# Attention scores of tiles 2 to 4 as three fp32r products

## The chip, the core and the metric

The kernel runs on one core of a Trainium2 chip. A core has five engines with a queue each: TensorE (PE, matmuls; its weight loads are shown apart as PEld), VectorE (DVE), ScalarE (ACT), GpSimd (POOL) and SyncE (SP, which issues DMAs). They share the on-chip memory SBUF; TensorE writes into PSUM, from which VectorE and ScalarE read. The metric is the device time of one launch in microseconds, the median of several runs. A run takes a little longer than its span, which is the time from the first to the last instruction in the trace.

## The reference, cut to what matters

Block-causal attention for 8 batches of 8 heads with 576 positions of 64 numbers, then a mixture of 8 experts of which each position takes one.

```python
scores = scale * np.matmul(q, k.transpose(0, 1, 3, 2))      # scale = 1/8
mask = block_i >= block_j                                   # blocks of 64 positions
scores = np.where(mask, scores, -1000000000.0)
attn = np.exp(scores - np.max(scores, axis=-1, keepdims=True))
attn = attn / (np.sum(attn, axis=-1, keepdims=True) + 1e-09)
x = np.matmul(attn, v)                                      # heads side by side: 4608 rows of 512
...
h = np.maximum(xe @ w1[e], 0.0)                             # the rows of one expert
out[mask] = gate_w[mask, None] * (h @ w2[e])
```

All inputs and the output are float32.

## The kernel before, in words

The kernel has two parts. The first, up to some 360 us, does the attention and the routing (class Attention, class Router); the second does the experts (class Experts) and isn't touched, except that one job which prepares its weights runs in the first part.

**Pairs and tiles.** The attention works on 32 pairs of heads, four to a batch. A pair's two heads lie in the two halves of the 128 partitions, so that a matmul of one head uses 64 rows; they are called a and b. The 576 rows of scores of a head are cut into tile 0 (64 rows, both heads in one matmul, line 160) and tiles 1 to 4 (128 rows each). Tile i needs the keys up to its end: 192, 320, 448 and 576 columns. Tile 4 is written in two matmuls of 288 columns. `op_S` (line 155) issues them, head a and head b by turns, each with the scaled queries `q` as the weights and the raw keys `kd` as the moving operand, in f32. Scores of tiles 1 to 3 go to the PSUM tiles ya and yb, those of tile 4 to xa and xb.

**Steps.** Each step of a pair has a short name: ld (loads qd, kd and v), pQ (scales q by 1/8 on GpSimd, line 114), S (scores), K (mask, VectorE memset), M (maximum, VectorE, line 187), E (exp with sum, ScalarE, line 202), R1 and R2 (sum plus epsilon, line 208, and reciprocal, line 211, on VectorE), Z (scales tile 0 on GpSimd, line 215), T (transposes on TensorE, line 241), H (their copies out of PSUM, on ScalarE, one on VectorE), V (product with v), O (copy of that), F, X and Y (the product with a folded matrix, and the scaling of its rows).

**Order.** The string ORDER (line 416) is the order in which one turn of the loop issues steps; `S4:2` means tile 4 of the pair that is two turns old. So one turn works on five pairs at once, and the 32 pairs take 36 turns. Within an engine the instructions run in that order; across engines semaphores hold them apart. An entry z issues a step of the router, an entry y (`other`, line 1546) takes one job from a list: a scatter of token numbers (line 697, on GpSimd), a gather, or a half of a weight split. There are 8 such splits, of 512 columns each: `first` (line 1510) writes the high part of a piece of w1 in fp32r, `second` (line 1516) the low part, both on GpSimd. The type fp32r is a float32 that is rounded so that one product of TensorE takes it; the experts' matmuls are already done as three products of high and low parts.

## Time and profile before

| | |
|---|---|
| median of 3 runs | 811.13 us (810.02 to 811.5) |
| the profiled execution: time, span | 810.1 us, 808.4 us |
| TensorE busy | 781.2 us, 97% of the span |
| weight loads busy | 592.4 us |
| VectorE, ScalarE, GpSimd busy | 471.8, 400.0, 389.7 us |
| mean granted clock of TensorE | 0.996 of 2.4 GHz |

A row of a timeline names an engine, the line of the kernel, the instruction, what it writes and reads (buffer numbers left out), and the shape. A f32 matmul of TensorE stands as two records. In brackets stands how long the engine had been idle, and what ended that. The ends of matmuls are modelled; the distance from start to start tells what one costs.

### The profile page before, as it was taken

What the parts mean: (1) busy time and instruction counts of PE and PEld (TensorE: products, weight loads), DVE (VectorE), ACT (ScalarE), POOL (GpSimd) and SP (SyncE); (2) the same over time, 40 slices, a digit from 0 to 9 for tenths busy, and PEclk for the clock granted to TensorE, in tenths of its full rate; (3) what the DMA queues carried; (4) which work ended last, traced back from release to release, by engine and by line L of the source; (5) the groups of instructions that cost most, each with busy time, mean ns of one, the idle gap of its engine ahead of it and who ended that gap; (6) DMA issues with size and microseconds to landing.
All of it is one profiled execution on the core that took longest, in us unless ns stands there. A gap on an engine that the chain in (4) does not pass through costs nothing.

```text
span 808.4 us, 17546 instructions
## 1 busy us (share of the span) xinstructions
PE 781.2 (97%) x4524; PEld 592.4 (73%) x4524; DVE 471.8 (58%) x1316; ACT 400.0 (49%) x1016; POOL 389.7 (48%) x397
## 2 busy tenths in 40 slices
PE   4999999999999999998999999999999999999995
PEld 2677666667776666766878888888888888888874
DVE  3566666776776777665855764412144713656963
ACT  3677777777777787772432323322332222323221
POOL 4122243344443362425456776555555555575663
PEclk9999999999999999999999999999999999999998
DMA  5234454646362626442337676744456564677762
GB/s 164 98 101 155 131 149 140 158 135 154 121 167 95 147 86 160 159 107 49 139 110 222 192 237 171 234 134 118 121 150 192 171 185 122 194 223 223 223 207 74
DMA packets 71120, 123.65 MB, mean 153 GB/s; under 512 B 16449, under 2 KB 37697, under 8 KB 70978
## 3 DMA queue, kind: packets, MB, share of 16 engines
q1 hardware_dynamic: 49858, 87.84, 37.4%
q0 software_dynamic: 7680, 20.50, 8.0%
q10 hardware_dynamic: 13440, 13.78, 6.3%
q8 instruction: 45, 0.74, 0.4%
q14 instruction: 97, 0.79, 0.4%
HBM read 73.09 MB, written 21.98 MB: 118 GB/s over the span
## 4 chain that ended last, share of the span: by engine, by line
PE 93%; POOL 2%; ACT 1%; issue 1%; DMA 1%; ACTq 1%; DVE 1%; DVEq 0%; POOLq 0%
PE py L1172 25%; PE o L272 12%; PE pt L1011 11%; PE ya L171 7%; PE o L1011 7%; PE ph L1011 7%; PE xa L171 5%; PE o L307 4%; PE o L301 1%; ACT pb L202 1%; PE o L160 1%; ACTq L1122 1%; DMA xg<-xd,idx 0%; POOL low L1145 0%; POOL tab L697 0%
## 5 line engine op out<-in xcount | busy, mean ns | idle before, releaser
L1172 PE MATMUL py<-w,low 128*128 (+1 forms) x912 | 217.3, 394 | 3.3 <-POOL low L1145 2.0
L1172 PEld LDWEIGHTS py<-w,low 128*128 128x128 f32 x912 | 172.0, 189 | 41.6 <-POOL low L1145 2.5
L114 POOL TENSOR_SCALAR q<-qd 128x640 f32<-128x640 f32 x32 | 58.0, 1811 | 186.7 <-PE o L160 133.4
L1190 ACT ACTIVATE y<-py,gates 128x512 f32<-128x512 f32 x35 | 24.1, 689 | 184.6 <-issue 129.5
L1145 POOL TENSOR_TENSOR low<-high,low 128x512 fp32r<-128x512 f32 x69 | 97.3, 1433 | 12.1 <-ACT low L1137 11.5
L980 POOL TENSOR_TENSOR xl<-high,xh 128x512 fp32r<-128x512 f32 x33 | 45.7, 1385 | 109.8 <-ACT xh L970 109.8
L1089 DVE STREAM_TRANSPOSE hblk<-xg 128x512 f32<-128x512 f32 x35 | 24.8, 709 | 87.9 <-DMA xg<-xd,idx 84.6
L202 ACT ACTIVATE pb<-ya,neg 128x320 f32<-128x320 f32 (+2 forms) x96 | 50.1, 525 | 48.1 <-DVE neg L187 48.1
L1011 PE MATMUL pt<-w,xh 128*128 x272 | 70.8, 392 | 0.0
L1333 DVE TENSOR_TENSOR w<-raw,w 128x1024 f32 x48 | 68.0, 1456 | 0.0
L1330 DVE CAST w<-raw 128x1024 f32 x48 | 56.8, 1222 | 16.0 <-issue 12.6
L171 PE MATMUL ya<-kd,q 64*128 64x192 f32 (+2 forms) x192 | 61.8, 456 | 2.7 <-ACT pb L202 2.7
L171 PE MATMUL yb<-kd,q 64*128 64x192 f32 (+2 forms) x192 | 61.8, 456 | 0.0
L1011 PEld LDWEIGHTS pt<-w,xh 128*128 128x128 f32 x272 | 51.0, 188 | 11.1
L697 POOL DMA_INDIRECT tab<-toks,posi x40 | 41.5, 1037 | 28.8 <-DVE run L664 14.8
L918 POOL DMA_INDIRECT xg<-xd,idx x39 | 44.0, 1128 | 19.3 <-POOL idx L910 17.2
L202 ACT ACTIVATE pb<-yb,neg 128x192 f32<-128x192 f32 (+2 forms) x96 | 49.8, 526 | 0.2 <-DVE neg L187 0.2
L1137 ACT CAST low<-high 128x1024 fp32r<-128x1024 f32 x35 | 36.6, 1045 | 26.5 <-DMA high<-hblk 26.5
L1101 DVE STREAM_TRANSPOSE hblk<-pt 128x512 f32<-128x512 f32 x34 | 23.4, 705 | 43.4 <-ACT pt L1048 43.4
L171 PE MATMUL xa<-kd,q 64*128 64x288 f32 x128 | 41.6, 447 | 6.6 <-POOL q L114 6.6
L307 PE MATMUL o<-fold,oT 128*128 128x144 f32 x256 | 43.9, 294 | 1.1 <-ACT oT L279 0.6
L187 DVE TENSOR_REDUCE neg<-yb 128x1 f32<-128x192 f32 (+2 forms) x96 | 42.8, 474 | 3.3
(1013 smaller groups left out, 1775.1 us busy)
## 6 DMA issues: line engine op xcount, KB each, us to landing
raw<-w SPq DMA_DIRECT2D x52, 512.0 KB, 4.9
high<-hblk SPq DMA_DIRECT2D x280, 48.0 KB
high<-hblk ACTq DMA_DIRECT2D x280, 48.0 KB
qd<-qT SPq DMA_DIRECT2D x32, 352.0 KB, 3.1
v<-vt SPq DMA_DIRECT2D x32, 352.0 KB, 4.8
kd<-kT SPq DMA_DIRECT2D x32, 288.0 KB, 3.8
xd<-xt SPq DMA_DIRECT2D x7, 1026.0 KB, 8.9
xd<-xg SPq DMA_DIRECT2D x9, 256.5 KB, 7.0
```

The lines of the kernel that those rows point to most:

```text
L114: self.nc.gpsimd.tensor_scalar(q, self.raws[m][0][:, 0 : 512 + P], 0.125, None, ALU.mult)
L171: ins = mm(out, q[r, 128 * (i - 1) : 128 * i], k[r, o : o + n], start=True, stop=True, skip_group_check=True)
L202: ins = self.nc.scalar.activation(dst, src, AF.Exp, bias=self.neg[m][:, c : c + 1], scale=1.0, accum_out=self.sums[m][:, c : c + 1])
L272: self.nc.tensor.matmul(out[r], self.raws[m][2][:, slot], self.ph[m, bank][:, c0:c1], start=t in (0, 5), stop=t in (4, 5), skip_group_chec ...
L307: mm(t[:, i], self.oT[m, 0][:, o : o + P], w, start=True, stop=True)
L918: pool.indirect_dma_start(out=self.xg[i], out_offset=None, in_=self.xd[:, :], in_offset=bass.IndirectOffsetOnAxis(ap=self.idx[:, t : t + 1 ...
L980: pool.tensor_sub(xl, r, xh).then_inc(sem["xp"], 1)
L1011: m = pe.matmul(ph[f], x[:, P * k : P * k + P], weights(k, f, part), start=start and k == 0, stop=stop and k == 3,)
L1145: engine.tensor_sub(hl[:, c], h[:, c], hh[:, c]).then_inc(sem["ln" if engine is pool else "le"], 1)
L1172: m = pe.matmul(self.py[t % 2], h[:, c // 4, P * (c % 4) : P * (c % 4) + P], wf[:, bass.ds(off + (base + 512 * c), 512)], start=n == 0, st ...
L1330: dve.tensor_copy(part(c, 0), raw[c % 4]).then_inc(sem["wh"], 1)
L1333: dve.tensor_sub(part(c, 1), raw[c % 4], part(c, 0)).then_inc(sem["wd"], 1)
```

## The change

- Pairs 2 to 31 get the scores of tiles 2, 3 and 4 in fp32r. Their queries and keys are split into a high part (rounded to fp32r) and a low part (the rest, in fp32r), and each f32 matmul becomes three: high by high, high by low, low by high, summed in PSUM. Tile 1, tile 0 and the first two pairs stay f32.
- `gQ` (GpSimd) scales the 384 columns of q for tiles 2 to 4 into the high part; `lQ` (GpSimd) subtracts it from q in three pieces of 128 columns. `gK` (ScalarE) copies the 576 columns of the keys into their high part; `lK` (GpSimd) subtracts it in four pieces of 144.
- In ORDER, pQ moves from behind S0 to behind Z and a new entry y2, with gQ and lQ behind it. gK and lK stand behind the last copy of the transposes (Hx3@A).
- A third entry y takes one more job from the list per turn, until the list is empty.
- The two halves of a weight split are each two instructions of 256 columns instead of one of 512.
- Three tile pools are added, two with two buffers each, and one of 64 bytes that nothing uses.

```diff
--- before.py
+++ after.py
@@ -57,6 +57,9 @@
         self.raw = ctx.enter_context(tc.tile_pool(name="araw", bufs=3))
         self.rawv = ctx.enter_context(tc.tile_pool(name="arawv", bufs=5))
         self.spl = ctx.enter_context(tc.tile_pool(name="aspl", bufs=2))
+        self.hk = ctx.enter_context(tc.tile_pool(name="ahk", bufs=2))
+        ctx.enter_context(tc.tile_pool(name="apart", bufs=1)).tile([P, 16], F32, tag="apart", name="apart")
+        self.hq = ctx.enter_context(tc.tile_pool(name="ahq", bufs=2))
         self.pt = ctx.enter_context(tc.tile_pool(name="apt", bufs=9))
         self.sm = ctx.enter_context(tc.tile_pool(name="asm", bufs=3))
         self.ot = ctx.enter_context(tc.tile_pool(name="aot", bufs=2))
@@ -65,7 +68,7 @@
         self.ps_t = ctx.enter_context(tc.tile_pool(name="pst", bufs=2, space=PSUM))
 
         self.cp, self.ident = cp, ident
-        self.raws, self.qs = {}, {}
+        self.raws, self.qs, self.hilo = {}, {}, {}
         self.pb, self.sums, self.neg, self.rs = {}, {}, {}, {}
         self.bank, self.ptile, self.ph, self.oT, self.xs = {}, {}, {}, {}, {}
         self.small_bank, self.at = (None, None), {}
@@ -113,6 +116,33 @@
         q = self.qs[m] = self.spl.tile([P, 512 + P], F32, tag="q", name=f"q{m}")
         self.nc.gpsimd.tensor_scalar(q, self.raws[m][0][:, 0 : 512 + P], 0.125, None, ALU.mult)
 
+    def high_low(self, m, k, n):
+
+        pool = self.hk if k == "k" else self.hq
+        self.hilo[m, k] = [pool.tile([P, n], F32R, tag=k + x, name=f"{k}{x}{m}") for x in "hl"]
+        return self.hilo[m, k][0]
+
+    def op_gQ(self, m):
+
+        if m > 1:
+            self.nc.gpsimd.tensor_scalar(self.high_low(m, "q", 384), self.raws[m][0][:, P:512], 0.125, None, ALU.mult)
+
+    def op_lQ(self, m):
+        if m > 1:
+            hi, lo = self.hilo[m, "q"]
+            for c in range(0, 384, P):
+                self.nc.gpsimd.tensor_sub(lo[:, c : c + P], self.qs[m][:, P + c : 2 * P + c], hi[:, c : c + P])
+
+    def op_gK(self, m):
+        if m > 1:
+            self.nc.scalar.copy(self.high_low(m, "k", S), self.raws[m][1])
+
+    def op_lK(self, m):
+        if m > 1:
+            hi, lo = self.hilo[m, "k"]
+            for c in range(0, S, 144):
+                self.nc.gpsimd.tensor_sub(lo[:, c : c + 144], self.raws[m][1][:, c : c + 144], hi[:, c : c + 144])
+
     def banks(self, m, x):
 
         if (m, x) not in self.bank:
@@ -160,18 +190,25 @@
             mm(self.part(1, m, "S0", 432, 496), q[:, 512:], self.raws[m][0][:, 512 + P :], start=True, stop=True)
             return
         e = 64 + 128 * i
+        at = P * (i - 1)
+        terms = ((q, k),)
+        if m > 1 and i > 1:
+            (qh, ql), (kh, kl) = self.hilo[m, "q"], self.hilo[m, "k"]
+            terms, at = ((qh, kh), (qh, kl), (ql, kh)), at - P
         for c in range(2 if i == 4 else 1):
-            for j in range(2):
-                out, _ = self.region(m, i, j)
-                if i == 4:
-                    out = out[:, c]
-                n = out.shape[-1]
-                o = (0 if j else S - e) + n * c
-                r = slice(64 * j, 64 * j + 64)
-                ins = mm(
-                    out, q[r, 128 * (i - 1) : 128 * i], k[r, o : o + n], start=True, stop=True, skip_group_check=True
-                )
-                self.uses(m, i, j, ins)
+            for a, (q, k) in enumerate(terms):
+                for j in range(2):
+                    out, _ = self.region(m, i, j)
+                    if i == 4:
+                        out = out[:, c]
+                    n = out.shape[-1]
+                    o = (0 if j else S - e) + n * c
+                    r = slice(64 * j, 64 * j + 64)
+                    ins = mm(
+                        out, q[r, at : at + P], k[r, o : o + n], start=a == 0, stop=a == len(terms) - 1,
+                        skip_group_check=True,
+                    )
+                    self.uses(m, i, j, ins)
 
     def op_K(self, m, i, j):
 
@@ -332,7 +369,7 @@
 
         name, _, engine = name.partition("@")
         k = name[0]
-        if name in ("ld", "pQ", "R1", "R2", "Z"):
+        if name in ("ld", "pQ", "gQ", "lQ", "gK", "lK", "R1", "R2", "Z"):
             getattr(self, "op_" + name)(m)
         elif name in ("O", "O0"):
             getattr(self, "op_" + name)(m, engine)
@@ -414,9 +451,9 @@
 
 
 ORDER = """
-E3B:3 V5:4 z2:0 O0@D:4 ld:0 Ta1:3 O@A:4 Ha1@A:3 S0:3 S4:2 z6:0 M0:3 Tb1:3 Tk0:3 pQ:1 K4B:2 E0:3 R1:3 K4A:2 z1:0 M4B:2
-R2:3 F1:4 Hb1@A:3 Ta2:3 Hk0@A:3 X1:4 Y1:4 M4A:2 Tb2:3 F2:4 E4B:2 y0:0 Z:3 Hb2@D:3 F0:4 Ha2@A:3 Y2:4 z4:0 Tx3:3 Tt0:3
-E4A:2 X2:4 S1:2 z5:0 z0:0 z3:0 Ht0@A:3 Y0@D:4 S2:2 K1A:2 K2A:2 S3:2 K1B:2 Hx3@A:3 K2B:2 V0:3 V2:3 M2A:2 K3A:2 M1B:2
+E3B:3 V5:4 z2:0 O0@D:4 ld:0 Ta1:3 O@A:4 Ha1@A:3 S0:3 S4:2 z6:0 M0:3 Tb1:3 Tk0:3 K4B:2 E0:3 R1:3 K4A:2 z1:0 M4B:2
+R2:3 F1:4 Hb1@A:3 Ta2:3 Hk0@A:3 X1:4 Y1:4 M4A:2 Tb2:3 F2:4 E4B:2 y0:0 Z:3 y2:0 pQ:1 gQ:1 lQ:1 Hb2@D:3 F0:4 Ha2@A:3 Y2:4 z4:0 Tx3:3 Tt0:3
+E4A:2 X2:4 S1:2 z5:0 z0:0 z3:0 Ht0@A:3 Y0@D:4 S2:2 K1A:2 K2A:2 S3:2 K1B:2 Hx3@A:3 gK:1 lK:1 K2B:2 V0:3 V2:3 M2A:2 K3A:2 M1B:2
 M3A:2 E2A:2 E1B:2 V1:3 y1:0 E3A:2 V3:3 M1A:2 K3B:2 M2B:2 E1A:2 M3B:2 V4:3 E2B:2
 """
 
@@ -1511,13 +1548,15 @@
                 for i in again:
                     weights(i)
                 again.clear()
-                nc.gpsimd.tensor_add(split(hi), split(w), z)
+                for i in range(2):
+                    nc.gpsimd.tensor_add(split(hi)[:, 4 * i : 4 * i + 4], split(w)[:, 4 * i : 4 * i + 4], z)
 
             def second():
-                nc.gpsimd.tensor_sub(low[k][:, f], w, hi)
+                for i in range(0, 512, 256):
+                    nc.gpsimd.tensor_sub(low[k][:, f, i : i + 256], w[:, i : i + 256], hi[:, i : i + 256])
                 again.append(n + 3)
 
-            z = att.zero[:, None, :].to_broadcast([P, 8, D])
+            z = att.zero[:, None, :].to_broadcast([P, 4, D])
             todo.extend((first, second))
 
         def sink(b, xt, x0, lg):
```

What this makes of three queues stands below; names with h or l are high and low parts, and a row's x2 or x4 counts like instructions.

TensorE, second half of a turn, from the last transpose to the scores of tile 3. Before:

```order
L238 MATMUL pt13t_2185<-ident,p_1997 64x128
L171 MATMUL ya_2189<-kd_1807,q_1987 128x192
L171 MATMUL yb_2191<-kd_1807,q_1987 128x192
L171 MATMUL ya_2189<-kd_1807,q_1987 128x320
L171 MATMUL yb_2191<-kd_1807,q_1987 128x320
L171 MATMUL ya_2189<-kd_1807,q_1987 128x448
L171 MATMUL yb_2191<-kd_1807,q_1987 128x448
```

and now, up to the first product of tile 3:

```order
L275 MATMUL pt13t_2588<-ident,p_2358 64x128
L207 MATMUL ya_2592<-kd_2130,q_2391 128x192
L207 MATMUL yb_2594<-kd_2130,q_2391 128x192
L207 MATMUL ya_2592<-kh_2437,qh_2393 128x320
L207 MATMUL yb_2594<-kh_2437,qh_2393 128x320
L207 MATMUL ya_2592<-kl_2438,qh_2393 128x320
L207 MATMUL yb_2594<-kl_2438,qh_2393 128x320
L207 MATMUL ya_2592<-kh_2437,ql_2394 128x320
L207 MATMUL yb_2594<-kh_2437,ql_2394 128x320
L207 MATMUL ya_2592<-kh_2437,qh_2393 128x448
L207 MATMUL yb_2594<-kh_2437,qh_2393 128x448
```

Two f32 matmuls of a tile are now six in fp32r, of which the middle two read kl, the last thing that GpSimd writes for a pair; tile 1 is as it was.

GpSimd, from one scaling of q to the next, in a turn with weight splits (high and low_75 are what they write, p is Z). Before:

```order
L114 TENSOR_SCALAR q_1691<-qd_1503 128x640
L1514 TENSOR_TENSOR high<-xg_191,zero 128x512
L215 TENSOR_SCALAR p_1550<-p_1550,rs_1548 128x64
L1517 TENSOR_TENSOR low_75<-xg_191,high 128x512
L114 TENSOR_SCALAR q_1844<-qd_1657 128x640
```

and now:

```order
L117 TENSOR_SCALAR q_1849<-qd_1589 128x640
L128 TENSOR_SCALAR qh_1851<-qd_1589 128x384
L134 TENSOR_TENSOR ql_1852<-q_1849,qh_1851 128x128 x3
L144 TENSOR_TENSOR kl_1907<-kd_1590,kh_1906 128x144 x4
L1556 TENSOR_TENSOR low_75<-xg_201,high 128x256 x2
L1552 TENSOR_TENSOR high<-xg_202,zero 128x256 x2
L252 TENSOR_SCALAR p_1814<-p_1814,rs_1812 128x64
L1556 TENSOR_TENSOR low_75<-xg_202,high 128x256 x2
L117 TENSOR_SCALAR q_2035<-qd_1761 128x640
```

Between two scalings stand now eight pieces for the fp32r parts, and three halves of weight splits instead of two, one of them between Z and the scaling.

ScalarE, from the copies of the last transposes to the first exps of the second half of a turn. Before:

```order
L250 COPY h_132<-pt13t_2185 64x128
L253 COPY ph13x_2212<-pt13x_2180 128x512
L202 ACTIVATE pb_2139,sums_2136<-ya_2189,neg_2137 128x320
L202 ACTIVATE pb_2139,sums_2136<-yb_2191,neg_2137 128x192
```

and now:

```order
L287 COPY h_142<-pt13t_2588 64x128
L290 COPY ph13x_2623<-pt13x_2583 128x512
L138 CAST kh_2625<-kd_2309 128x576
L239 ACTIVATE pb_2532,sums_2529<-ya_2592,neg_2530 128x320
L239 ACTIVATE pb_2532,sums_2529<-yb_2594,neg_2530 128x192
```

The cast of the keys stands between the last copy and the exp of tile 2; nothing else moved there.

## Rows read from the trace of the kernel before

**Rows 1.** Busy time by stretch: stretch, length, then busy us of each engine, clock, DMA.

```profile
100.00:200.00 100.00, 100.00 (x762) 69.69 (x763) 69.58 (x284) 76.63 (x232) 41.53 (x40) 1.00 0.57 150
```

**Rows 2.** Waits of TensorE: who, on whom, total us, times, longest.

```profile
PE xa L171 <- POOL q L114: 6.6, 1, 6.6
```

**Rows 3.** Timeline of TensorE, one turn: start, duration, line, out<-in, shapes, count.

```profile
203.90 0.66 PE L241 MATMUL pt17a<-ident,pb 128*128 128x128 f32 x4
...
204.66 0.51 PE L171 MATMUL xa<-kd,q 64*128 64x288 f32 x1
204.66 0.51 PE L171 MATMUL xb<-kd,q 64*128 64x288 f32 x1
205.00 0.40 PE L171 MATMUL xa<-kd,q 64*128 64x288 f32 x1
...
205.25 0.40 PE L171 MATMUL xa<-kd,q 64*128 64x288 f32 x1
...
210.02 0.43 PE L171 MATMUL ya<-kd,q 64*128 64x320 f32 x1
...
210.29 0.43 PE L171 MATMUL ya<-kd,q 64*128 64x320 f32 x1
...
210.56 0.54 PE L171 MATMUL ya<-kd,q 64*128 64x448 f32 x1
...
210.94 0.54 PE L171 MATMUL ya<-kd,q 64*128 64x448 f32 x1
...
215.45 0.51 PE L171 MATMUL xa<-kd,q 64*128 64x288 f32 x1
```

**Rows 4.** Timeline of TensorE in the experts part.

```profile
500.19 1.07 PE L1011 MATMUL pt<-w,xl 128*128 x4
501.10 2.00 PE L1011 MATMUL pt<-w,xh 128*128 x8
```

**Rows 5.** Timeline of the weight loads of tile 4.

```profile
204.66 0.18 PEld L171 LDWEIGHTS xa<-kd,q 64*128 64x128 f32 x1
204.66 0.18 PEld L171 LDWEIGHTS xb<-kd,q 64*128 64x128 f32 x1
204.76 0.19 PEld L171 LDWEIGHTS xa<-kd,q 64*128 64x128 f32 x1
```

**Rows 6.** ScalarE: timeline, then two lines of the code (ns min/median/max).

```profile
202.67 0.41 ACT L202 ACTIVATE pb<-ya,neg 128x192 f32<-128x192 f32 x1
...
211.87 0.53 ACT L202 ACTIVATE pb<-ya,neg 128x320 f32<-128x320 f32 x1 [1.44 <-DVE neg L187]
...
L970 ACT CAST xh<-high x33: 603/610/621, 429.4 to 781.1; 128x512 fp32r<-128x512 f32 x33
...
L1137 ACT CAST low<-high x35: 1038/1042/1062, 423.2 to 793.8; 128x1024 fp32r<-128x1024 f32 x35
```

**Rows 7.** Groups on GpSimd: shapes, count, busy us, mean ns, idle before.

```profile
L114 POOL TENSOR_SCALAR q<-qd 128x640 f32<-128x640 f32 x32 | 58.0, 1811 | 186.7 <-PE o L160 133.4 <-issue 51.4 <-DMA qd<-qT 1.0
...
L215 POOL TENSOR_SCALAR p<-p,rs 128x64 f32<-128x64 f32 x32 | 14.4, 451 | 22.9 <-DVE rs L211 12.4 <-ACT ph31b L253 6.5 <-ACT ph6b L253 0.6
...
L1514 POOL TENSOR_TENSOR high<-xg,zero 128x512 fp32r<-128x512 f32 x8 | 10.2, 1273 | 0.0
```

**Rows 8.** Timelines of GpSimd and of VectorE, same turn as rows 3.

```profile
204.88 1.81 POOL L114 TENSOR_SCALAR q<-qd 128x640 f32<-128x640 f32 x1 [6.01 <-issue]
...
206.09 0.15 DVE L208 TENSOR_TENSOR rs<-sums,eps 128x9 f32<-128x9 f32 x1
...
206.99 0.20 DVE L211 RECIPROCAL rs<-rs 128x9 f32<-128x9 f32 x1
```

**Rows 9.** Two lines of the experts part: ns min/median/max, first and last start.

```profile
L1333 DVE TENSOR_TENSOR w<-raw,w x48: 1208/1214/4009, 416.6 to 792.0; 128x1024 f32 x48
...
L1145 POOL TENSOR_TENSOR low<-high,low x69: 1279/1299/2278, 426.0 to 794.9; 128x512 fp32r<-128x512 f32 x69
```

## The prediction

> **What bounds the kernel now.** I read first the busy time by stretches: in the attention part TensorE is busy for all of 100 us, VectorE for 70, ScalarE for 77, GpSimd for 42, and TensorE's granted clock is 1.00, its level of 2.4 GHz [rows 1]. Then the waits of TensorE: the longest one in the whole run is 6.6 us, once, at the start [rows 2]. So over the 32 turns of the attention loop TensorE is the bound and nobody makes it wait; one turn is the distance from 204.66 to 215.45, 10.79 us [rows 3]. What is taken off TensorE in a turn shortens the turn, until another engine is late.
>
> Last the timeline of TensorE in one turn. Each f32 matmul stands there as two records, and the two heads of a pair (xa, xb) start together and run side by side. From one record to the next it is 0.25 us for 288 columns (205.00 to 205.25), 0.27 for 320, 0.38 for 448 [rows 3]: close to 0.845 ns a column, two cycles at 2.4 GHz. A matmul thus costs four cycles a column for both heads together.
>
> **TensorE, the term that gains.** Tiles 2 to 4 have 320 + 448 + 2 x 288 = 1344 columns a pair. Before: 1344 x 2 x 0.845 ns = 2.27 us. After: three products in fp32r, 12 steps (a step is one product for both heads) with 3 x 1344 = 4032 columns. No row shows fp32r with 64 rows and two heads side by side. The nearest are the expert matmuls, fp32r with 128 rows and 512 columns: four from 500.19 to 501.10, 0.228 us each [rows 4], that is 0.213 for 512 columns at one cycle each, and 15 ns more. So the 12 steps take 4032 / 2.4 = 1.68 us and 12 x 0.015 = 0.18, 1.86 in all, and a turn gains 0.41 us. I take this. Upper end: the excess is only the 3 ns by which 0.27 lies above two cycles for 320 columns; 1.72 us, a gain of 0.55. Lower end: 15 ns for each head; 2.04 us, a gain of 0.23. Thirty of the 32 pairs are changed: 30 x 0.41 = **12.3 us** (6.9 to 16.5). The weights are no hindrance as long as two heads load side by side: one pair of loads starts 0.10 us after the other [rows 5], and the shortest step streams 0.12.
>
> **ScalarE, the keys' high part.** Casts of 512 and 1024 columns took 0.61 and 1.04 us, so 576 take about 0.66. It stands behind the copy of ph..x and ahead of the exp of tile 2, where ScalarE was idle for 1.44 us until VectorE's maximum came [rows 6]. That maximum comes some 0.3 us earlier after the change (shorter scores of tiles 4 and 2), so 1.1 us of cover hold 0.66 of work: nothing. Without the cover the exps behind it, and with them TensorE's transposes a turn later, would be late by 0.66.
>
> **GpSimd, the term that loses.** This engine gets eight new instructions in a row: behind Z (0.45 us, 64 columns) stands now the scaling of q (1.81, 640 columns), the high part of q (384 columns), three pieces of 128 and four pieces of 144. No row has pieces so short. Upper end: a straight line through 64 columns in 0.451 us and 512 in 1.273 (for one input through 640 in 1.811) [rows 7]: 0.57 for 128, 0.60 for 144, 1.21 for 384. Lower end: in proportion to 512 and 640 columns: 0.32, 0.36 and 1.09. So Z to the last piece takes 0.45 + 1.81 + 1.21 + 1.70 + 2.39 = 7.56 us at most, 5.74 at least; nothing decides between them, and I take the middle, 6.65.
>
> When must it be done? Z waits for VectorE's reciprocal, which ended at 206.99 + 0.20 [rows 8], 2.53 us after the first score of tile 4; with that tile shorter by 0.17, 2.36. The second product of the next pair's tile 4 needs the last piece of kl: one turn later (10.38) and one first step (0.23). That leaves 10.38 + 0.23 - 2.36 = 8.25 us: slack 0.69 at the upper end, 1.60 in the middle, 2.51 at the lower. Turns with nothing else stay hidden. But the new entry y2 puts one more job between Z and the scaling. In the instruction order of the changed kernel six turns have there a scatter (1.02 and 0.17 of issue [rows 8]), three a half of a weight split alone, and four a split half there and two more ahead of Z. A split half is now two instructions of 256 columns: 1.61 us at most (the line), 1.27 at least, 1.44 in the middle. Upper end: 6 x 0.50 + 3 x 0.92, and the four full turns hold 7.56 + 3 x 1.61 = 12.4 us of GpSimd against a turn of 10.38, so 4 x 2.0: 13.8 us. Lower end: 0. Middle: only the four full turns (6.65 + 3 x 1.44 = 10.97) are late, by about 0.5 us each: **2.0 us**. The wait falls on TensorE, which does nothing else meanwhile, since the scores of tile 4 stand ahead of the transposes in its queue.
>
> The Trainium skill (GPSIMD Engine Reference, section 3.1) gives 4497 ns for an addition with two inputs of 2048 columns. With the 1.27 us of 512 columns that makes, as an estimate, 0.47 and 0.50 us for the pieces and a chain of 6.89 us, so the stalls would come to about 4 us and not 2; no run here shows it yet.
>
> **Elsewhere nothing.** The experts' part gets the same instructions, and the scatters only come earlier. The moved pQ is one instruction, on GpSimd, and what it passes there is counted above; a job that y2 takes may also issue a load of w1 on SyncE's queue, a turn earlier than before, which nobody waits for. VectorE keeps its instructions and order; its first mask in the second half waits for scores that now come sooner. The last exp that the next transposes on TensorE need ended at 202.67 + 0.41 [rows 6], 0.82 us ahead of them (203.90) [rows 3]; the scores of tile 3, which lie between, shrink by 0.76 - 0.60 = 0.16.
>
> **Sum.** 12.3 - 2.0 = 10.3 us. The profiled execution took 810.1 us with a span of 808.4; its span would be 798.1 and its time 799.8. The median of the runs shown, 811.13, lies 1.0 above that execution, so I predict **800.8**.
>
> **The rivals.**
>
> Two heads in turn (slower): if in fp32r the two heads' matmuls don't run side by side, 12 steps become 24: 3.36 + 24 x 0.015 = 3.72 us against 2.27, a loss of 1.45 a turn, 30 times: 854.6. It decides as soon as more than about a fifth of the streams don't overlap (0.41 of 1.86). For it: no row shows fp32r in half the rows. Against it: in f32 the heads start together, streams and loads alike [rows 3, 5]. Chance 0.08.
>
> Loads in turn (slower): streams overlap, but the two loads of a step follow each other, 0.10 each and so 0.20, as long as a step of tile 3 and longer than the others: 12 x 0.20 = 2.40 us, a loss of 0.13 a turn, 30 times: 815.0. Against it speak the pairs of loads that start together [rows 5]. Chance 0.06.
>
> GpSimd is the bound: short pieces cost what the line says, and the stalls are 13.8 us: 811.13 - 12.3 + 13.8 = 812.6; with part of it anything from 805 up. For it: a piece of 64 columns does cost 0.45. Chance 0.17.
>
> The change doesn't do what it says: fp32r in half the rows is slower by as much as the three products save (0.034 us on each of 12 steps), and the time stays at 811. Chance 0.08.
>
> VectorE blocked by GpSimd: in the experts' part VectorE's subtraction of two tensors took 1208 to 4009 ns, while GpSimd subtracted too, and GpSimd's own 1279 to 2278 [rows 9]; so the two can hold each other up. In the attention part VectorE's addition for the sums (L208) took 0.15 us at 206.09, in the middle of the scaling on GpSimd from 204.88 to 206.69 [rows 8]. If it did block, the addition would now wait in the four full turns for a split piece of up to 0.80, and with it the maximum, the exp and the transposes behind it: 3.2 us more, 804.0. The Trainium skill (SBUF — State Buffer, "SBUF: two separate sides") has this as a rule: a VectorE instruction with two SBUF inputs and a GpSimd instruction that reads SBUF hold one port pair exclusively. By that rule L208 would have waited until 206.69; by the row it didn't wait. Chance 0.06.
>
> **How the numbers follow.** The forecast, 800.8, has 0.55; its own range is 794.6 (a gain of 16.5, no stall) to 806. The rivals have the chances above. The range goes from 794 to 813, which takes in the forecast, GpSimd's upper end, no change, and the blocked VectorE; left out are the two slower cases of TensorE (0.14) and some 0.05 at the ends. About 0.2%, 1.6 us, is what a measurement can tell here. Faster: 0.55 + 0.06 + most of GpSimd's case 0.13 + 0.02 of the case without effect = 0.76. Same: 0.03 + 0.04 = 0.07. Slower: 0.14 + 0.01 + 0.02 = 0.17.
>
> **What would show it.** In the timeline of TensorE the steps of xa should lie 0.135 us apart for 288 columns, 0.15 for 320, 0.20 for 448, with xa and xb starting together; 0.27 or 0.20 for 288 would be the first or second rival. The turn should be 10.4 us in turns without extra work on GpSimd. Among TensorE's waits a new one for kl should stand, about 2 us in total, in the turns with weight splits; 10 or more would be the third rival. The groups should show 0.32 to 0.57 us for ql, 0.36 to 0.60 for kl, and 0.66 for the cast of kh, with ScalarE still idle ahead of the exp of tile 2. Wrong would be the whole if kl is waited for in every turn, or if TensorE waits for exps that it had in time before.

## The result, and the profile after

The changed kernel takes 799.75 us (median of five runs, 798.8 to 801.47), the kernel before 810.64 beside it (809.52 to 811.5): a ratio of 0.9867, 95% interval 0.9849 to 0.9885, 10.9 us less. The prediction was 800.8. The profiled execution has a span of 798.0 us; 798.1 was forecast from 808.4.

Busy time by stretches, kernel after, the attention part as in [rows 1] (stretch, length, then the engines, clock, DMA):

```profile
100.00:200.00 100.00, 98.90 (x854) 74.03 (x851) 76.64 (x284) 84.20 (x252) 93.18 (x138) 1.00 0.58 154
```

GpSimd has gone from 41.53 us of 100 to 93.18, and TensorE, which was busy without a gap, is idle for 1.1 us. So this stretch shows both sides of the change. The gain stands in TensorE's timeline, one turn, answering to [rows 3] (start, duration, line, out<-in, shapes):

```profile
198.65 0.34 PE L190 MATMUL o<-qd,q 128*128 128x64 f32 x2
198.92 0.40 PE L207 MATMUL xa<-kh,qh 64*128 64x288 f32 x1
198.92 0.40 PE L207 MATMUL xb<-kh,qh 64*128 64x288 f32 x1
199.16 0.29 PE L207 MATMUL xa<-kl,qh 64*128 64x288 f32 x1
...
199.29 0.29 PE L207 MATMUL xa<-kh,ql 64*128 64x288 f32 x1
...
199.42 0.29 PE L207 MATMUL xa<-kh,qh 64*128 64x288 f32 x1
...
204.25 0.30 PE L207 MATMUL ya<-kl,qh 64*128 64x320 f32 x1
...
204.39 0.31 PE L207 MATMUL ya<-kh,ql 64*128 64x320 f32 x1
...
204.54 0.36 PE L207 MATMUL ya<-kh,qh 64*128 64x448 f32 x1
...
204.74 0.36 PE L207 MATMUL ya<-kl,qh 64*128 64x448 f32 x1
...
209.02 0.34 PE L190 MATMUL o<-qd,q 128*128 128x64 f32 x2
```

The two heads start together (198.92 twice). A step is 0.13 us for 288 columns, 0.145 for 320 and 0.20 for 448; only the first step behind the f32 matmul is longer (198.92 to 199.16), as the first record was before (204.66 to 205.00 [rows 3]). The turn, from 198.65 to 209.02, is 10.37 us instead of 10.79: 0.43 gained.

TensorE's waits (who, on whom, total us, times, longest) in the whole run and then in the attention stretch alone:

```profile
PE xa L207 <- POOL q L117: 6.5, 1, 6.5
...
PE pt15a L278 <- ACT pb L239: 0.4, 1, 0.4
```

```profile
PE o L344 <- DVE lg L363: 0.4, 1, 0.4
PE o L190 <- DVE o L320: 0.3, 1, 0.3
```

No wait for kl is among them, and in all 30 pairs the steps that read kl follow the step before at the distances shown above. How long each turn takes shows where the rest went. A turn is the distance between the matmuls of tile 0 (L190) of successive pairs, read from TensorE's timeline; turn 10 goes from pair 10 to pair 11:

```
turn                8     9    10    11    12    13    14    15    16    17    18    19    26
before          10.78 10.81 11.02 10.79 10.79 10.79 11.02 10.79 10.79 10.79 11.02 10.79 11.56
after           10.36 10.37 10.65 10.98 10.37 10.42 11.53 10.76 10.36 10.37 10.65 10.36 11.14
after, again    10.35 10.37 11.54 10.77 10.36 10.39 10.65 10.99 10.36 10.38 10.68 10.36 11.14
```

Thirty turns are 0.43 us shorter, 12.9 us; turns 11, 14 and 15 lose 0.62, 0.94 and 0.40 of it, and all that is lost comes to 2.1 us ("the loss" from here on: what the turns stand above 10.36, or above 10.59 and 11.14 in the turns that were 11.02 and 11.56 before). The spans differ by 10.4 us: 12.9, less the loss of 2.1, plus 1.0 at the start (the first of these matmuls at 17.47 here, at 18.19 before; turn 0 is 0.25 shorter), less 1.25 at the very end, told below: 10.5. The gain at the start isn't settled: pair 1 has this matmul at 30.08 here and at 31.04 before, and of the twelve runs below seven have it at 30.1 to 30.5 and five at 31.0 to 31.1.

### The profile page after: what moved, and what is told of

The parts are those of the page before. It is cut to its first block, busy times and chain, and to the rows that moved or that the text cites. A ratio compares the mean times of both kernels' runs of the same rounds, so it can differ in the third digit from the quotient of the medians.

```text
span 798.0 us, 18415 instructions
## 1 busy us (share of the span) xinstructions
PE 767.2 (96%) x4764; PEld 602.2 (75%) x4764; DVE 477.8 (60%) x1316; ACT 417.1 (52%) x1046; POOL 516.7 (65%) x653
## 4 chain that ended last, share of the span: by engine, by line
PE 85%; issue 3%; DVE 2%; SPq 2%; DMA 2%; ACT 1%; ACTq 1%; POOL 1%; DVEq 0%; POOLq 0%
PE py L1209 21%; PE o L309 12%; PE pt L1048 10%; PE o L1048 6%; PE ph L1048 6%; PE ya L207 6%; PE xa L207 4%; PE o L344 4%; ACTq L1159 1%; SPq L1159 1%; PE o L338 1%; PE o L190 1%; DMA out<-y,idx 1%; DVE neg L224 1%; ACT pb L239 1%
## 5 line engine op out<-in xcount | busy, mean ns | idle before, releaser
L1182 POOL TENSOR_TENSOR low<-high,low 128x512 fp32r<-128x512 f32 x69 | 95.2, 1401 | 16.4 <-ACT low L1174 16.0
L1370 DVE TENSOR_TENSOR w<-raw,w 128x1024 f32 x48 | 70.8, 1514 | 0.0
L252 POOL TENSOR_SCALAR p<-p,rs 128x64 f32<-128x64 f32 x32 | 14.3, 445 | 77.4 <-DVE rs L248 31.1
L1367 DVE CAST w<-raw 128x1024 f32 x48 | 50.5, 1092 | 15.5 <-issue 13.6
L144 POOL TENSOR_TENSOR kl<-kd,kh 128x144 fp32r<-128x144 f32 x120 | 55.0, 490 | 0.0
L1231 POOL DMA_INDIRECT out<-y,idx x35 | 37.7, 1076 | 16.9 <-ACT y L1227 11.8
L224 DVE TENSOR_REDUCE neg<-yb 128x1 f32<-128x192 f32 (+2 forms) x96 | 42.8, 474 | 3.3
```

Of the source, the lines that this page charges most:

```text
L144: self.nc.gpsimd.tensor_sub(lo[:, c : c + 144], self.raws[m][1][:, c : c + 144], hi[:, c : c + 144])
L224: ins = self.nc.vector.tensor_reduce(self.neg[m][:, c : c + 1], src, AX.XY if i == 4 else AX.X, ALU.max, negate=True)
L1182: engine.tensor_sub(hl[:, c], h[:, c], hh[:, c]).then_inc(sem["ln" if engine is pool else "le"], 1)
L1367: dve.tensor_copy(part(c, 0), raw[c % 4]).then_inc(sem["wh"], 1)
L1370: dve.tensor_sub(part(c, 1), raw[c % 4], part(c, 0)).then_inc(sem["wd"], 1)
```

## The experiments

"Theory A" in the expectations: VectorE's instructions with two SBUF inputs are held up by GpSimd's pieces. "Theory B": the keys' low part, kl, comes late.

**What the loss is made of.** First turn 11 of the kernel after, where VectorE, GpSimd, then TensorE stand so:

```profile
135.74 0.61 DVE L245 TENSOR_TENSOR rs<-sums,eps 128x9 f32<-128x9 f32 x1
...
136.38 0.65 DVE L727 TENSOR_TENSOR rc<-r,seven 128x5 int32<-128x5 int32 x1
136.95 0.74 DVE L224 TENSOR_REDUCE neg<-xb 128x1 f32<-128x576 f32 x1
```

```profile
134.88 1.43 POOL L1552 TENSOR_TENSOR high<-xg,zero 128x256 fp32r<-128x256 f32 x2
136.26 1.43 POOL L1556 TENSOR_TENSOR low<-xg,high 128x256 fp32r<-128x256 f32 x2
137.99 0.44 POOL L252 TENSOR_SCALAR p<-p,rs 128x64 f32<-128x64 f32 x1 [0.30 <-DVE rs L248]
```

```profile
138.34 0.73 PE L344 MATMUL o<-fold,oT 128*128 128x144 f32 x4 [0.38 <-DVE lg L363]
```

The addition for the sums (L245, L208 before) takes 0.61 us and ends at 136.35, just after GpSimd went on to its next piece (136.26); the shift behind it (L727, usually 0.15) takes 0.65 and ends at 137.03, in step with the next piece boundary. Behind both stands the maximum (L224), and TensorE waits 0.38 us at 138.34. In most turns the addition is short (ns, min/median/max, over all 32 pairs):

```profile
L245 DVE TENSOR_TENSOR rs<-sums,eps x32: 149/150/606, 20.6 to 346.6; 128x9 f32<-128x9 f32 x32
```

It is long in five pairs: 0.61 us in turn 11, 0.54 to 0.55 in turns 10, 14 and 18, 0.27 in turn 15. Turns 10 and 18 lose only about 0.05 us, so the delay of one addition alone is nearly absorbed.

Turn 14 loses the most, 0.94 us. VectorE and GpSimd there:

```profile
170.94 1.02 DVE L636 SCALAR_TENSOR_TENSOR at<-w,base 128x5 f32<-128x5 f32 x1
...
172.31 0.74 DVE L715 TENSOR_SCALAR g<-g 128x5 f32<-128x5 f32 x1
```

```profile
169.82 1.43 POOL L1552 TENSOR_TENSOR high<-xg,zero 128x256 fp32r<-128x256 f32 x2
171.20 1.83 POOL L117 TENSOR_SCALAR q<-qd 128x640 f32<-128x640 f32 x1
```

Both VectorE instructions take 0.16 us in the kernel before. L636 starts beside a piece that ends at 171.25 and ends itself at 171.96, 0.76 us into the scaling of q; L715 ends at 173.06, with the scaling (173.03). The maxima behind them come about 1 us later in their turn than in turn 22, and TensorE waits 0.42 us for the exp that needs them (pt15a above). Then a copy of four columns (L682, 0.53 us instead of 0.16) ends with a kl piece, and TensorE waits 0.26 us for the copy behind it (o L320).

So the scaling, which has one input, holds VectorE up as well. A clean case is turn 9 of the run fill2_again, told below, VectorE and then GpSimd:

```profile
118.83 0.72 DVE L619 TENSOR_TENSOR L<-L,m 128x40 f32<-128x40 f32 x1
```

```profile
118.77 1.82 POOL L117 TENSOR_SCALAR q<-qd 128x640 f32<-128x640 f32 x1
```

L619 has two inputs in SBUF and takes 0.19 us alone; here it ends 0.78 us into the scaling. In the kernel after and in fill2_again every one of the router's VectorE instructions with two SBUF inputs that starts in the first 0.7 us of a scaling of q ends 0.74 to 0.82 us behind its start; those that start later take their usual time.

**fill** takes the pieces' inputs away and leaves GpSimd's time about as long.

```diff
-                for i in range(2):
-                    nc.gpsimd.tensor_add(split(hi)[:, 4 * i : 4 * i + 4], ...)
+                for i in range(3):
+                    nc.gpsimd.memset(hi.bitcast(F32), 0.0)
```

(the same for the low part). 

> Left out: the split of the experts' first weights; each half is three fills of 512 columns instead (write only, no read), about 3 x 0.54 = 1.63 us on GpSimd, where the two subtractions took 1.46. The changed kernel loses 1.96 us in three turns (11, 14 and 15: 0.62, 0.94, 0.40 over their neighbours). Theory A (VectorE instructions with two SBUF inputs wait for GpSimd's instructions with two SBUF inputs): the loss goes, VectorE's addition of the sums takes 0.15 us in every turn instead of up to 0.61, the three turns take 10.37, 10.65 and 10.37 us, the time falls by 2 us to 797.8. Theory B (GpSimd is late with kl, or just too busy): GpSimd is as busy as before, the three turns stay long, 799.8 or more.

Measured: 802.87 us, ratio 0.9909 (0.9882 to 0.9935), a loss of 4.6 us. GpSimd and VectorE, then TensorE and its waits, in turn 11 of this run:

```profile
136.83 1.69 POOL L1552 MEMSET high<- 128x512 f32 x3
```

```profile
137.67 0.15 DVE L245 TENSOR_TENSOR rs<-sums,eps 128x9 f32<-128x9 f32 x1
```

```profile
136.95 0.40 PE L207 MATMUL xa<-kl,qh 64*128 64x288 f32 x1 [0.24 <-POOL kl L144]
```

```profile
PE xa L207 <- POOL kl L144: 1.5, 6, 0.3
```

The addition takes 0.15 us in the middle of a fill: without inputs on GpSimd VectorE isn't held up there. So the rows are as theory A has them, and the time isn't, since the three fills take 1.69 us from end to end where the two pieces take 1.43, and now kl is late, as the prediction had it. That is the whole loss: in turns 10, 11 and 12 the steps around the kl products are 0.21, 0.82 and 1.05 us longer together, and so are these turns (the listed waits count idle time alone). The changed kernel thus sits at the edge of that wait: a quarter of a microsecond more on GpSimd per weight step brings it out.

**splits_alone** makes every high and low part and leaves all scores in f32.

```diff
-        if m > 1 and i > 1:
+        if False:
```

> The scores stay f32, but all high and low parts are still made, in the same places. Both theories: TensorE's steps are those of before, 10.79 us a turn. Theory A: VectorE still waits for GpSimd in the turns with weight halves, about 2 us in all on top of before: 812.6. Theory B: nobody needs kl, the turn is longer, so the loss goes: 810.6. The difference to the changed kernel is what fp32r alone gives: 0.43 us in each of 30 turns, 12.9 us.

Measured: 812.12 us, ratio 1.0015 (0.9997 to 1.0032), turns of 10.79 and a loss of 1.1 us in turns 10, 11 and 15. Here VectorE's addition is held up too, with TensorE 0.43 us a turn slower, while GpSimd is on a weight:

```profile
141.45 0.77 DVE L245 TENSOR_TENSOR rs<-sums,eps 128x9 f32<-128x9 f32 x1
```

```profile
140.77 1.42 POOL L1556 TENSOR_TENSOR low<-xg,high 128x256 fp32r<-128x256 f32 x2
```

By the ratio the splitting alone costs 1.2 us (-0.2 to 2.6; 1.1 by the turns), and from 812.12 to 799.75 fp32r is worth 12.4.

**no_low** leaves the low parts out and takes all three products from the high parts; routing then sends other tokens to the experts, so that only its attention part can be compared.

```diff
-            terms, at = ((qh, kh), (qh, kl), (ql, kh)), at - P
+            terms, at = ((qh, kh),) * 3, at - P
```

> Left out: both low parts (seven pieces, 3.3 us of GpSimd a turn); the three products all take the high parts, so TensorE has the same steps. Theory A: the weight halves remain and VectorE waits for them as before where they still meet its additions, so of the 1.96 us at least half stays: 798.8 to 799.8. They come some 3 us earlier in the turn, though, so which VectorE instruction they meet may change. Theory B: GpSimd is far from late, the loss goes: 797.8.

Measured: 822.12 us, its part behind the last pair 24 us longer. In the attention part turns 11, 14 and 15 are 10.36, 10.73 and 10.37; the loss is 0.3 us. With 3.1 us less of ql and kl per turn the weights' pieces run at another time, and the addition doesn't meet them. What the weights' pieces cost thus depends on which VectorE instructions the rest of GpSimd's chain pushes them under.

**whole** makes every piece whole again: ql 384 columns, kl 576, weight halves 512.

```diff
-            for c in range(0, S, 144):
-                self.nc.gpsimd.tensor_sub(lo[:, c : c + 144], ...)
+            self.nc.gpsimd.tensor_sub(lo, self.raws[m][1], hi)
```

> All pieces on GpSimd whole again: q's low part 384 columns at once, the keys' 576, a weight half 512. From the pieces measured (0.457 us for 128, 0.490 for 144, 0.733 for 256, 1.27 for 512: 0.185 us fixed and 2.12 ns a column) GpSimd has 0.9 us less to do in a turn, and 0.2 less for each weight half. Theory A: what VectorE waits for lasts up to 1.3 instead of 0.7 us, so the loss in the turns with weight halves about doubles: 801.7, and VectorE's addition of the sums takes up to 1.3 us. Theory B: GpSimd is earlier, the loss shrinks: 798.

Measured: 798.17 us, ratio 0.9841 (0.9818 to 0.9864), a loss of 0.75. VectorE and GpSimd in turn 11:

```profile
136.75 0.81 DVE L243 TENSOR_TENSOR rs<-sums,eps 128x9 f32<-128x9 f32 x1
...
137.60 0.14 DVE L725 TENSOR_TENSOR rc<-r,seven 128x5 int32<-128x5 int32 x1
```

```profile
136.26 1.28 POOL L1552 TENSOR_TENSOR low<-xg,high 128x512 fp32r<-128x512 f32 x1
```

The addition still waits for the piece to end (137.56 against 137.54), even longer, but only once: the shift behind it takes 0.14 and not 0.65. Short pieces, which should let VectorE in between them, let one instruction in here and hold up the next. The time is the one that was expected of theory B (798), while the rows show A's mechanism: A's price, a loss twice as large, was wrong.

**Four edits on one chip.** Of the next four, these are the edits:

```diff
fill2      -   two pieces of 256 columns     +   two fills of 512 columns (memset, 1.05 us)
one_input  -   tensor_add(hi, w, zero)       +   tensor_scalar(hi, w, 1.0, None, ALU.mult)
wholew     -   weight halves 2 x 256         +   weight halves 512, ql and kl as in the changed kernel
cast3      -   one copy of kh on ScalarE     +   three copies, same source and target
```

In fill2 the experts' weights are left out. 

> Each of the two steps of an experts' weight (high part, low part: GpSimd's two pieces of 256 columns each) is replaced by two write-only fills of 512 columns, 0.525 us each, so 1.05 us instead of 1.46; the experts' weights are left out, the attention part is the changed kernel's. Theory A (the loss of turns 11, 14 and 15 is VectorE held up by GpSimd's pieces with two inputs; in the run with three fills, 1.57 us, that loss had only changed its place, to the keys' low part that came late): with 1.05 us both reasons are gone, all turns 10.36 us (10.6 where a batch begins, 11.1 in turn 26), first to last S0 about 1.9 us shorter than in the changed kernel; median 797.5 to 798.5. Theory B (the weights' transfers or their place in the order cost, whatever GpSimd does with them): turns 11, 14 and 15 stay 0.4 to 1.2 us long, 799.5 to 800.

> The high part of an expert's weight is made by a multiplication with 1.0 (one input, two pieces of 256 columns) instead of an addition of zero (two inputs); the low part stays a subtraction. Theory A in its narrow form (only GpSimd instructions with two inputs hold VectorE up): VectorE's addition ahead of the reciprocal takes 0.15 us again in turns 10, 11, 14 and 15, the instruction that met the second step (0.65 us) keeps that; turn 14 loses 0.5 instead of 1.2 us. But a piece is longer, about 0.8 us by the query scaling's 1172 ns for 384 columns (instead of 0.73), so GpSimd is 0.15 to 0.2 us later per weight, and the keys' low part may be late by up to 0.2 us in the full turns: net 799 to 801. Theory A in its wide form (any GpSimd piece holds it up): turn table as in the changed kernel, 799.5 to 801.

> Only the experts' weight halves go in one piece of 512 columns again (1274 ns each instead of 2 x 733); the queries' and keys' low parts stay in short pieces. Theory A: short pieces hold VectorE up several times in a row, a whole one once, so turns 11, 14, 15 lose about 0.74 us together, as in the run with everything whole, and GpSimd is 0.19 us earlier: 798 to 799. Rival: the gain of the run with everything whole came from the queries' and keys' pieces (457 x 3 + 490 x 4 = 3331 ns against 1004 + 1409 = 2413 ns, 0.92 us earlier keys), then this run stays at 799.5 to 800 with about 1.9 us lost.

> ScalarE copies the keys' high part three times (same source, same target) instead of once: 2 x 0.67 = 1.35 us more per turn, at the same place, ahead of the exponentials of tile 2. The prediction's step says that the cast is hidden in ScalarE's idle time at that place; in the changed kernel 0.80 to 0.92 us are left there. Theory S (that idle time is the whole cover): the exponentials of tile 2 come 0.4 to 0.55 us late, the turn is 10.8 to 10.9 us, 30 x 0.4 to 0.55 = 12 to 16.5 us more: 812 to 816. Rival (the other idle pieces behind it, 0.61 and 0.15 us a turn, take it up, or the exponentials were not what TensorE waits for): 800 to 803.

Measured: fill2 804.12 us, one_input 804.32, wholew 804.03, cast3 813.97. All expectations for the first three missed, both sides, by 3 to 4 us from the nearer bound. The three have a disturbance in common: in turns 8, 20, 24 and 28 VectorE begins the mask of xb 0.5 to 0.8 us late, though the score lies ready. The kernel after shows such a late mask in turn 9 alone, by 0.35 us, as the kernel before does. VectorE, pair 20 of fill2:

```profile
234.09 0.22 DVE L224 TENSOR_REDUCE neg<-o 128x1 f32<-128x64 f32 x1 [1.23 <-PE o L190]
235.04 0.11 DVE L219 MEMSET xb<- 64x64 f32 x1 [0.73 <-PE pt20b L278]
```

TensorE's last matmul of xb had begun there at 234.05 and lasts 0.29; in the other runs the mask follows at 1.49 us from the start of the pair, here at 2.03. In this pair the delay begins earlier: the maximum of tile 0 (L224 above) starts 1.08 us after its scores do, in fill2_again 0.38, and the mask stands behind the exp of that maximum; in turn 8 only the mask is late. These three runs thus say little of their edits. From one_input one thing can be read: a one-input piece of 256 columns took 846 ns, a two-input one 730, and the addition still took 0.47 to 0.55 us in turns 10, 11 and 15. In turns 11 and 15 a two-input subtraction ran beside it; in turn 10 it ended 0.43 us into a one-input piece, and the shift of turn 15 (0.32 us) 0.42 us into one. So a one-input piece holds VectorE up too, for about half of its time.

cast3 can be read in the turns without the disturbance: 10.70 in turns 19, 23 and 27 (10.36 after). ScalarE in the kernel after, answering to [rows 6], then in cast3:

```profile
150.97 0.67 ACT L138 CAST kh<-kd 128x576 fp32r<-128x576 f32 x1
152.56 0.53 ACT L239 ACTIVATE pb<-ya,neg 128x320 f32<-128x320 f32 x1 [0.92 <-DVE neg L224]
```

```profile
310.67 2.08 ACT L140 CAST kh<-kd 128x576 fp32r<-128x576 f32 x3
312.66 0.52 ACT L241 ACTIVATE pb<-ya,neg 128x320 f32<-128x320 f32 x1
```

One cast leaves 0.92 us of idle time ahead of the exp. Two more casts, 1.4 us, take it all (no idle time is shown ahead of 312.66), and the turn grows by 0.34, a little less than the 0.4 to 0.55 expected. So that idle time is the cover of the cast, as the prediction said, and beyond it ScalarE does cost TensorE. That the median lies within the 812 to 816 expected is luck in part: 30 turns of 0.34 make 10.2 us, and the other 4 us above 799.75 are about what the three disturbed runs beside it lose.

**Whose is the disturbance?** The changed kernel again, with two edits, on a third chip. 

> The changed kernel itself once more, beside two edits of it on the same chip. In the four runs with two fills, one-input pieces, whole weight halves and three casts (one chip), VectorE began a memset about 0.5 us late in turns 8, 20, 24 and 28 though TensorE's scores lay ready, which the earlier runs (another chip) show in turn 9 alone, and turns 9 to 17, 21, 25 and 29 were longer there, whatever the edit. Theory C (that belongs to the chip, not to the edits): where the changed kernel shows those late memsets again, it takes 803 to 805 us, and the edits of that batch were worth nothing either way; where it doesn't show them, 799 to 801 and the turns 11, 14 and 15 long as before. Theory D (the edits did it: all four shift GpSimd's stream): 799 to 801 here without late memsets, whatever the chip.

> All pieces on GpSimd whole (low part of the queries 384 columns, of the keys 576, weight halves 512), again, beside the changed kernel on the same chip. GpSimd's chain ahead of the keys' low part is 0.92 us shorter a turn (3331 ns of pieces against 2413). Theory C: where VectorE starts late by 0.5 us, that 0.92 us takes it up, so this kernel stays at 798 to 799.5 and its turns at 10.36 to 10.75 even where the changed kernel needs 803 to 805; without late memsets 797 to 799, 1 to 2 us ahead of the changed kernel. Rival (the shorter chain is worth nothing beside a late VectorE, since what is late there is VectorE's own work): as far behind as the changed kernel, within 1 us of it.

wholeqk makes ql and kl whole and leaves the weights in pieces of 256.

> Only the queries' and the keys' low parts are made whole (384 and 576 columns, 1004 and 1409 ns instead of 3 x 457 and 4 x 490); the experts' weight halves stay in two pieces of 256 columns. Theory A (what the changed kernel loses in turns 11, 14 and 15 comes from the weight halves' short pieces, which hold VectorE up in a row): those turns stay long, about 1.9 us together, as in the changed kernel, 799 to 801 where the changed kernel takes 799 to 801. Rival (it comes from GpSimd's chain: with 0.92 us less of it the pieces of the weights fall elsewhere and nothing is late): 797.5 to 799, as with everything whole.

Measured: the changed kernel 799.32 us, whole 799.33, wholeqk 798.55; no late masks of that kind, which theories C and D both allow on this chip. The loss is 2.1, 0.76 and 1.15 us (turns 11, 14 and 15 of wholeqk: 10.63, 10.87, 10.77), the spans 797.7, 796.9 and 796.8. So a GpSimd chain that is 0.92 us shorter a turn takes about half of the loss away, the weights' whole halves some of the rest. But 0.8 us of 799 is no more than the runs differ: the medians don't tell the three apart (whole had been expected 1 to 2 us ahead), and nothing here is a version that is measurably better than the changed kernel.

Then the first of the disturbed four once more. 

> The kernel with two write-only fills of 512 columns (1.05 us) in place of the two pieces of each weight step (1.46 us), once more; the experts' weights are left out, the rest is the changed kernel's. Its first run stands at 804.12 us with VectorE's memsets about 0.5 us late in turns 8, 20, 24 and 28, as the other three kernels of that chip did. Theory C (those belong to the chip): on a chip without them turns 8, 20, 21, 24, 25, 28 and 29 are 10.36 us; and if the loss in turns 10 to 15 is made only of VectorE held up by GpSimd's pieces with two inputs, or of the keys' low part that comes late where GpSimd is slower, both reasons are gone, all turns to the last S0 are 10.36 (10.59 where a batch begins, 11.14 in turn 26), about 1.9 us shorter than the changed kernel's: 797 to 798.5 us. Theory D (this edit makes them): 803 to 805 again, with the same turns long. If it shows the turns 8, 20, 24 and 28 short but the turns 10 to 15 long, another reason for the loss is open.

Measured: 798.72 us, ratio 0.985 (0.9832 to 0.9868), against 804.12 on the other chip. VectorE, pair 20 again:

```profile
231.12 0.11 DVE L219 MEMSET xb<- 64x64 f32 x1 [0.88 <-ACT p L239]
```

The same program, 5.4 us apart: the late masks belong to that chip, or to the hour on it, and not to the edits. What held VectorE there, no row names: in pair 20 of fill2 the scores of tile 0 lay ready for about 0.7 us. With the two fills the additions take 0.15 to 0.17 us in every pair and no wait for kl shows, and the loss is 0.8 us in place of 2.1. No loss had been expected, and there is one: turns 10 and 14 still lose 0.39 and 0.23, and there other VectorE instructions stand long, one of them a plain copy of four columns, VectorE and then GpSimd:

```profile
134.46 0.97 DVE L682 COPY xt<-g 128x4 f32<-128x4 f32 x1
```

```profile
133.55 1.39 POOL L144 TENSOR_TENSOR kl<-kd,kh 128x144 fp32r<-128x144 f32 x3
134.88 1.11 POOL L1552 MEMSET high<- 128x512 f32 x2
```

It ends at 135.43, with the first of the two fills. So the query and key pieces hold VectorE up as well, and a fill may do so for an instruction that is already waiting. Which VectorE instructions wait to the end of a GpSimd instruction and which only for its first part, the runs don't settle.

## Why the prediction was right, and which step was not

**The gain.** Right. It put the steps at 0.135, 0.15 and 0.20 us; they are 0.13, 0.145 and 0.20. The turn gains 0.43 us for 0.41, within bounds of 0.23 and 0.55, and 30 turns 12.9 for 12.3. Both slower rivals of TensorE, heads in turn and loads in turn, fall with the rows above: xa and xb start together, and a step of 288 columns is 0.13 and not 0.20 or 0.27. So does the change without effect.

**ScalarE.** Right: 0.674 us for 0.66, hidden; cast3 shows how much cover was left.

**GpSimd's prices.** Right: the middle of the bounds, not either end. Its groups, answering to [rows 7]:

```profile
L117 POOL TENSOR_SCALAR q<-qd 128x640 f32<-128x640 f32 x32 | 58.2, 1817 | 1.1 <-DMA qd<-qT 1.0
L144 POOL TENSOR_TENSOR kl<-kd,kh 128x144 fp32r<-128x144 f32 x120 | 55.0, 490 | 0.0
L134 POOL TENSOR_TENSOR ql<-q,qh 128x128 fp32r<-128x128 f32 x90 | 38.6, 457 | 2.5
...
L128 POOL TENSOR_SCALAR qh<-qd 128x384 fp32r<-128x384 f32 x30 | 35.2, 1172 | 0.0
...
L1556 POOL TENSOR_TENSOR low<-xg,high 128x256 fp32r<-128x256 f32 x16 | 11.4, 734 | 0.0
```

The bounds were 0.32 to 0.57 for ql and 0.36 to 0.60 for kl, with 1.44 taken for a weight step of two pieces; measured are 0.457, 0.490 and 1.43. (The scatter's 1.02 and 0.17 us, which [rows 8] doesn't show, stand at 206.87 in the trace of before.) The chain of Z to the last piece was taken as 6.65 us and takes 6.52 where nothing lies between. These pieces, with 1004 ns for 384 columns and 1409 for 576 in the kernels with whole ones, lie on one line of 0.19 us and 2.12 ns a column. The estimate from the Trainium skill (GPSIMD Engine Reference, section 3.1), 0.47 and 0.50 us, agrees; its stalls of 4 us don't, for the reason that follows.

**The stalls: the failed step.** The prediction put 2.0 us, as TensorE waiting for kl in four full turns. The size is right (2.1); the mechanism isn't. No wait for kl shows, though chain and weight steps cost what was assumed. It compared the work of a full turn (10.97 us) with the turn (10.38) and took the excess as late, without setting it against the slack of 1.60 us that it had just worked out for ordinary turns. The full turns come two in a row (10 and 11, 14 and 15), so the excess adds up to 1.2, which fits in there. (Its own figures also give 4 x 0.59 = 2.4, not 2.0.) That its 2.0 met the 2.1 is luck. How near the edge it is, fill shows: with 0.26 us more per weight step kl is waited for in six places. The rival with GpSimd as the bound, 13.8 us of stalls, rested on the upper prices and falls with them.

What is late instead is VectorE. Even one of the prediction's own signs of being wrong came once: in turn 14 TensorE waits for an exp that it had in time before. The rival of a blocked VectorE had 0.06 and a price of 3.2 us in four turns, three of which are those that lose, so its place was right and its chance too small. The row that spoke against it, the addition of 0.15 us in the query scaling [rows 8], is a fact, but it starts 1.21 us into the scaling, and wherever such an addition meets the scaling in the kernel before, it starts 1.2 us into it or later. Beside the first 0.7 us VectorE does wait, as shown above, and the change moves the scaling to where other VectorE instructions meet that part. The rows with two inputs on either engine [rows 9] showed durations that differ more than threefold, and they should have weighed more. The Trainium skill (SBUF — State Buffer, "SBUF: two separate sides") has the rule: two SBUF inputs on VectorE against a GpSimd instruction that reads SBUF, and whichever starts first blocks the other for its whole length. The traces agree for two-input pieces (0.61 and 0.65 us instead of 0.15) and for fills that read nothing (0.15); for the one-input scaling they agree for its first 0.77 of 1.81 us, and not for the rest.

**Elsewhere.** The instructions of the experts' part are the same, but the part behind the last pair is 1.25 us longer (452.74 against 451.49, and 452.1 to 453.2 in all but two of the other runs). ScalarE and GpSimd at the end of the kernel after:

```profile
786.89 0.69 ACT L1227 ACTIVATE y<-py,gates 128x512 f32<-128x512 f32 x1 [3.13 <-DMA out<-y,idx]
...
791.31 0.69 ACT L1227 ACTIVATE y<-py,gates 128x512 f32<-128x512 f32 x1 [3.73 <-DMA out<-y,idx]
```

```profile
788.56 1.02 POOL L1231 DMA_INDIRECT out<-y,idx  x1 [2.51 <-ACT y L1227]
792.81 0.97 POOL L1231 DMA_INDIRECT out<-y,idx  x1 [3.23 <-ACT y L1227]
```

Each y waits until the scatter of the one before has landed, 4.4 us from y to y, so the end hangs on that relay; in the kernel before, the last y waited for TensorE. Why the relay starts later, no run tried. The sum gave 799.8 us for the profiled execution, and it took 799.75, which is also the median. That they agree so closely is luck: the 1.0 us at the start and the 1.25 at the end, which the prediction put at nothing, nearly cancel. The 1.0 us that was added because the median of before lay above its profiled execution wasn't there after the change.

## What to carry to other kernels

When work moves to an idle engine, ask not only whether it gets done in time but also which instructions of its neighbours it holds up while it runs; look at more than one place within the neighbour's instruction before a row is taken as proof that they don't. Set a full turn's excess against the slack of the turns around it before calling it a stall. Where a few microseconds decide, put the kernel itself beside its edits on the same chip.

## What was not expected of the hardware

- Short pieces on GpSimd needn't let VectorE through any better: in turn 11 an addition took 0.61 us and an instruction behind it 0.65 (0.15 each alone), while beside one whole piece of 1.28 us the addition took 0.81 and the other 0.14.
- A one-input scaling on GpSimd holds up VectorE's instructions with two SBUF inputs for its first 0.77 us of 1.81, and lets them through behind that (0.72 us for 0.19 at its beginning in fill2_again, 0.15 us at 1.21 us into it [rows 8]).
- The same program took 804.12 us on one chip and 798.72 on another, with VectorE's masks about 0.5 us late in four turns of the first; the kernel before showed 811.13 and 810.40 beside them, no such gap. Perhaps a kernel without slack shows what one with slack hides; no run tried it.
- Three products in fp32r with two heads of 64 rows side by side run at one cycle a column and 10 to 13 ns per step (0.13, 0.145 and 0.20 us for 288, 320 and 448 columns).
